# Sums of the exponentials in SBUF instead of PSUM, and a new hand-over to the list planner

## The chip, the cores and the metric

The kernel runs on one core of one Trainium2 chip. The metric is the device time of one execution in microseconds; the median over runs is given. TensorE (PE in the profile, PEld for its weight loads), VectorE (DVE), ScalarE (ACT), GpSimd (POOL) and the DMA queue of SyncE (SP) work side by side and wait for each other on semaphores.

## The reference, cut to what matters

Three layers follow each other. The first is attention on pooled keys and values (8 batches, 8 heads, 576 tokens, head size 64; 8 neighbouring keys are averaged, so 72 are left):

```
k_p = k.reshape(B, H, 72, 8, D).mean(axis=3); v_p = the same of v
scores = (q @ k_p^T) / 8;  scores -= max(scores)
attn = exp(scores);  attn /= (sum(attn) + 1e-9);  out = attn @ v_p
```

Its output, 4608 tokens of 512 numbers, passes two dense layers of 512 to 2048 to 512: `leaky(x @ w_in) @ w_out` with slope 0.01, and then `h * clip(h + 3, 0, 6) / 6` between two more such products. Each fp32 operand of these products is split into a high and a low part, so that three matmuls give one product.

## The kernel before, in words

The work is written as a list of tasks (`plan.add`, L130), each with an engine, an estimated cost in ns, a function that emits its instructions, and the views that it reads and writes. `Plan.order` (L211) makes each engine's instruction order out of it with a list schedule: twelve rounds forward and backward over the estimated costs and lags, of which the one with the earliest estimated end is kept. The estimates make the order alone; on the chip every wait is a semaphore. Copies among the first `flex` tasks (L303 to L314) may go to ACT or to DVE, as the schedule finds. `soon` (L1430) gives the first three weight chunks an earlier rank. Buffers of one tag rotate in the order in which the tasks are written down, whatever order the planner finds, and that is where the table `C` (L31) comes in: its `when`, `att`, `gaps`, `prep` and `left` numbers are slots, counted in steps of the dense layers, at which attention parts and weight preparation are written down between the steps.

Attention is done in 24 units, three per batch. A unit is, in this order: `scores` (L466: 24 or 32 small matmuls into two PSUM banks of tag `a`; the second unit's go to `y2` and `y3`), per bank a maximum on DVE (L503) and six exponentials on ACT (L512, 72 keys each, written to an SBUF tile `s` or `sb`), then 1e-9 added to the twelve sums (L523), their reciprocal (L524), and two products with it (L530 for the last 8 keys, L543 for the other 64). After that come `transposes` (L569) and `transpose_rem` (L587), whose results ACT and DVE split (`th`, `tl`, `rem`, `tr`), and `values` (L619), again into banks of tag `a`, of which there are two. Each exponential also writes the sum of its row (`accum_out`): in the profile that is a second ACT instruction, ACTIVATION_READ_ACCUMULATOR. Before the change it writes into columns 440 to 451 of the unit's first score bank.

The run has four parts. A ramp of some 35 us loads and pools keys and values and does the first two units; there the PE is kept running with matmuls on zeros (L1600, `idle`). Then the first dense layer takes three tiles of 512 tokens with plain products (`moe_tile`, L745 to L796), then three pairs of tiles (`Pair1`), then the second dense layer takes five pairs of 460 or 462 tokens. Both kinds of pair use seven products for eight (`Pair`, matmuls at L1049): 56 steps of six matmuls in `first`, then 56 steps in `second`, 112 slots in all. Their right sides are prepared by `prepare_some` (L1118), products 0 and 1 at one slot and 2 to 6 at another; their left sides are weights combined by DVE and ACT (`combine`, L948, `split_off`, L927) and kept in DRAM (`left`). The 24 units of attention are spread over the tiles and the first two pairs, and all have been done by 645 us. All loads and stores are issued from the one SP queue, in the planner's order.

Of the kernel before, what the change touches and what calls it, by code (L numbers as in the profile page):

```python
# [10 lines left out]
F32 = mybir.dt.float32  # L11
# [12 lines left out]
HALF, CQ, NC = 384, 128, 3  # L24
# [5 lines left out]
ROUNDS = 12  # L30
C = dict(  # L31
    n32=3,
    soon={0: 6000, 1: 6000, 2: 8000},
    flex=441,
    mid=8,
    half0=3,
    steps0='rfrfffrf',
    when0=[0, 2, 0, 8, 0, 10, 18],
    att0=[0, 14, 44],
    sec0=3,  # L40
    half1=3,
    steps1='frrfffrfffffffff',
    when1=[12, 20, 13, 22],
    att1=[0, 25, 31],
    sec1=3,
    att2=[7],
    quick=[0, 2, 0, 2, 3],
    slow=[0, 0, 5, 5, 3],
    left1=[[(0, 0), (1, 9)], [(2, 3), (3, 2)]],
    att3=[0, 5, 9, 12, 18, 22],  # L50
    gaps3=[0, 1, 1, 3, 2],
    prep3=[22, 31],
    att5=[9, 19, 32, 43, 54, 62],
    gaps5=[0, 4, 7, 9, 6],
    prep5=[82, 99],
    att7=[0, 16, 36],
    gaps7=[1, 10, 10, 12, 8],
    prep7=[72, 96],
    left2=[[(0, 11)], [(1, 15)], [(2, 27)], [(3, 39), (4, 43), (5, 61)], [(6, 17), (7, 30)]],
)  # L60
SCORES = 1500
EXPS = 1560
TRANSPOSES = 300
FIRST_LOADS = 1.25
WARM_FROM = 2700
ENGINES = ("pe", "act", "dve", "gp", "dma")
# [45 lines left out]
class Plan:  # L112
# [17 lines left out]
    def add(self, engine, cost, emit, reads=(), writes=(), other=None):  # L130

        n = len(self.tasks)
        after = set()
        over = lambda d, key: (t for k, v in d.items() if all(a == b for a, b in zip(k, key)) for t in v)
        for v in (*reads, *writes):
            assert not v.buf.gone, v.buf.name
            if v.buf.prev is not None:
                after |= v.buf.prev.users
        for v in reads:
            before = {t for key in v.keys for t in over(v.buf.writers, key)}  # L140
            assert before, v.buf.name
            after |= before
        for v in writes:
            for key in v.keys:
                after.update(over(v.buf.writers, key))
                after.update(over(v.buf.readers, key))
        after.discard(n)
        for v in reads:
            for key in v.keys:
                v.buf.readers.setdefault(key, set()).add(n)  # L150
            v.buf.users.add(n)
        for v in writes:
            for key in v.keys:
                v.buf.writers.setdefault(key, set()).add(n)
            v.buf.users.add(n)
        self.tasks.append(([(engine, cost, emit)] + ([other] if other else []), after))
# [97 lines left out]
def attention_moe_moe(ctx: ExitStack, tc: tile.TileContext, qt, kt, vm, vr, wt, wq, eye, mask, out):  # L254
# [14 lines left out]
    PE, ACT, DVE, GP, DMA = nc.tensor, nc.scalar, nc.vector, nc.gpsimd, nc.sync  # L269
    plan = Plan()  # L270
    add = plan.add

    def buf(tag, shape, dtype=F32, bufs=1, pool=sbuf):
        return Buf(plan, pool, tag, shape, dtype, bufs)
# [4 lines left out]
    def wide(ap, n):  # L279
        return ap.rearrange("p (a o) -> p a o", o=1).to_broadcast([ap.shape[0], ap.shape[1], n])  # L280
# [4 lines left out]
    def dve_cost(n, fast=False):  # L285
        return n / (1.92 if fast else 0.96) + 68
# [4 lines left out]
    def on_dve(n, emit, reads, writes, fast=False):  # L291
        add("dve", dve_cost(n, fast), emit, reads, writes)
# [4 lines left out]
    def on_pe(n, emit, reads, writes):  # L297
        add("pe", n, emit, reads, writes)
# [17 lines left out]
    def subtract(dst, a, b, n):  # L316
        on_dve(
            n,
            lambda: DVE.tensor_tensor(out=dst.ap(), in0=a.ap(), in1=f32(b.ap()), op=ALU.subtract),  # L319
            [a, b],  # L320
            [dst],
        )
# [9 lines left out]
    keys = [buf(f"keys{g}", [128, 2, SP])() for g in range(2)]  # L332
# [133 lines left out]
    def scores(u):  # L466


        assert all(held_keys[g] == u.b for g in u.groups)
        s = buf(u.tag, [128, 1024])  # L470
        u.rem = buf("rem", [CQ, NC, 3, 32], F32R, 2)
        mx = buf("mx", [CQ, NC, 4], F32, 2)
        at = lambda: s.get()[:, 0 : NC * 4 * SP].rearrange("p (c h k) -> p c h k", c=NC, h=4)
        tags = u.banks or [("a", 2), ("a", 2)]
        pss = [buf(tag, [128, 512], F32, bufs, psum) for tag, bufs in tags]
        if u.n == 2:
            blocks = [(slice(0, 128), c, c, 128 * c) for c in range(2)]
            blocks += [(slice(64 * g, 64 * g + 64), 2, g, 256 + 64 * g) for g in range(2)]
        else:
            blocks = [(slice(0, 128), c, u.g, 128 * c) for c in range(NC)]  # L480

        def emit():
            for to, c, g, at_ in blocks:
                for pi in range(2):
                    for e, ps in enumerate(pss):
                        rows = slice(64 * e, 64 * e + 64)
                        PE.matmul(
                            out=ps.get()[to, (2 * c + pi) * SP : (2 * c + pi) * SP + SP],
                            lhsT=u.q.ap()[rows, pi * HALF + at_ : pi * HALF + at_ + to.stop - to.start],
                            rhs=keys[g].ap()[rows, pi, :],  # L490
                            start=True,
                            stop=True,
                        )

        on_pe(SCORES, emit, [u.q, *(keys[g] for g in u.groups)], [ps("s") for ps in pss])
        sums = [pss[0](("m", e), lambda t, e=e: t[:, 440 + e : 452 + e]) for e in range(2)]
        for e, ps in enumerate(pss):
            s4 = lambda ps=ps: ps.get()[:, 0:432].rearrange("p (c a k) -> p c a k", c=NC, a=2)
            m = mx(e, lambda t, e=e: t[:, :, e : e + 3 : 2])

            on_dve(
                432,
                lambda m=m, s4=s4: DVE.tensor_reduce(out=m.ap(), in_=s4(), op=ALU.max, axis=AX.X, negate=True),  # L503
                [ps("s")],
                [m],
            )

            def exps(e=e, s4=s4):
                for c in range(NC):
                    for pi in range(2):  # L510
                        h = 2 * pi + e
                        ACT.activation(  # L512
                            out=at()[:, c, h, :],
                            in_=s4()[:, c, pi, :],
                            func=AF.Exp,
                            bias=mx.get()[:, c, h : h + 1],
                            accum_out=pss[0].get()[:, 440 + 4 * c + h : 440 + 4 * c + h + 1],
                        )

            add("act", EXPS, exps, [ps("s"), m], [s(e), sums[e]])  # L520
        whole = [s(pi) for pi in range(2)]
        inv = buf("inv", [CQ, 12], F32, 2)()
        on_dve(12, lambda: DVE.tensor_scalar_add(inv.ap(), pss[0].get()[:, 440:452], 1e-9), sums, [inv])  # L523
        add("dve", 144, lambda: DVE.reciprocal(out=inv.ap(), in_=inv.ap()), [inv], [inv])  # L524
        s3 = lambda: at().rearrange("p c h k -> p (c h) k")

        rn = buf("rn", [CQ, 12, 8], F32, 2)()
        on_dve(
            96,
            lambda: DVE.tensor_tensor(out=rn.ap(), in0=s3()[:, :, 64:SP], in1=wide(inv.ap(), 8), op=ALU.mult),  # L530
            [*whole, inv],
            [rn],
        )
        src = View(rn.buf, None, lambda t: t.rearrange("p (c h) k -> p c (h k)", c=NC))
        part = [u.rem(i, lambda t, i=i: t[:, :, i, :]) for i in range(3)]
        copy(part[0], src, 96)
        subtract(part[1], src, part[0], 96)
        copy(part[2], src, 96)

        flat = lambda: s.get()[:, 0 : NC * 256]  # L540
        on_dve(
            768,
            lambda: DVE.tensor_tensor(  # L543
                out=flat().rearrange("p (a k) -> p a k", k=64), in0=s3()[:, :, 0:64], in1=wide(inv.ap(), 64), op=ALU.mult
            ),
            [*whole, inv],
            whole,
        )
        u.p = lambda c, pi: flat()[:, 256 * c + 128 * pi : 256 * c + 128 * pi + 128]
        u.whole = whole  # L550
# [9 lines left out]
    def transposes(u):  # L560
        u.t = []
        pss = []
        for pi in range(2):
# [6 lines left out]

            on_pe(TRANSPOSES, emit, [*u.whole, ident], [ps()])
        for pi, ps in enumerate(pss):
# [9 lines left out]
    def transpose_rem(u):  # L582
# [9 lines left out]

        on_pe(TRANSPOSES, emit, [u.rem(), ident], [ps()])
        u.tr = buf("tr", [96, HALF], F32R, 1)()
# [46 lines left out]
    left1 = []  # L641
# [158 lines left out]
    class Jobs:  # L800
# [5 lines left out]
        def at(self, slot, *jobs):  # L806
            self.d.setdefault(slot, []).extend(jobs)
# [105 lines left out]
    left2 = Left(2)  # L913
# [487 lines left out]
    for u in units[: C["n32"]]:  # L1401
        g = u.n % 2
# [6 lines left out]
    for g in range(2):  # L1409
        for t in vbd[g]:  # L1410
            t = t()
# [251 lines left out]
```

## Time and profile before

| what | value |
|---|---|
| median of 3 runs | 1600.15 us (1599.05 to 1602.92) |
| time of the profiled execution | 1602.77 us |
| span of the profiled execution, first to last instruction | 1601.0 us |
| outside the span | 1.77 us |
| PE busy | 1575.8 us (98%) |
| DVE busy | 1159.1 us (72%) |
| ACT busy | 991.0 us (62%) |
| granted TensorE clock | 1.00 in every slice |

A busy PE is one with a matmul in flight; matmuls overlap, so busy time is not work. The chain that ended last is followed back from the last instruction, at each step to whatever released it. Idle time of an engine is listed with the instruction that ended it. In a timeline row the two first numbers are the start and the duration in us.

### The profile page before, as it was taken

How to read it: one execution, taken by the hardware profiler on the slowest of the kernel's cores; microseconds unless marked ns; L12 is line 12 of the kernel's file. 1: busy time of each engine (PE TensorE's matmuls, PEld its weight loads, DVE VectorE, ACT ScalarE, POOL GpSimd, SP SyncE). 2: the span in 40 equal slices, each digit the busy share in tenths (PEclk: the TensorE clock that was granted, in tenths of full speed). 3: DMA queues.
4: the chain of work that ended last, by engine and by line, in shares of the span. 5: the costliest groups of instructions: out<-in, count | busy, mean ns of one | idle time of the engine just before them, and what ended most of it. 6: DMA issues, size and time to landing. Idle time of an engine off the chain costs nothing.

```text
span 1601.0 us, 23002 instructions
## 1 busy us (share of the span) xinstructions
PE 1575.8 (98%) x8048; PEld 1348.6 (84%) x8048; DVE 1159.1 (72%) x2001; ACT 991.0 (62%) x2235; POOL 2.1 (0%) x12
## 2 busy tenths in 40 slices
PE   9999999999999999999999999999999999999999
PEld 8888878777787777778888889988888888898888
DVE  6987768568869966897577569658855955885494
ACT  7876765678876677666656455546545544654454
POOL 0000000000000000000000000000000000000000
PEclk9999999999999999999999999999999999999999
DMA  7789768649886799879987556856765685676564
GB/s 274 293 313 329 242 236 275 222 161 315 290 301 215 252 311 309 302 263 321 325 291 254 186 210 245 273 208 222 273 231 210 228 275 210 224 246 226 206 236 151
DMA packets 128323, 406.33 MB, mean 254 GB/s; under 512 B 18512, under 2 KB 47312, under 8 KB 106448
## 3 DMA queue, kind: packets, MB, share of 16 engines
q1 hardware_dynamic: 128208, 404.87, 73.2%
q8 instruction: 64, 1.05, 0.3%
q14 instruction: 51, 0.42, 0.1%
HBM read 317.79 MB, written 87.03 MB: 253 GB/s over the span
## 4 chain that ended last, share of the span: by engine, by line
PE 72%; DVE 12%; ACT 7%; DMA 6%; issue 2%; SPq 0%; ACTq 0%; DVEq 0%
PE y L1049 29%; PE h L1049 17%; PE a L1049 12%; ACT s L512 4%; DMA left<-st 3%; DVE w L916 2%; PE y L794 2%; PE y L796 2%; PE y L795 2%; PE a L619 2%; PE h L747 1%; PE h L746 1%; PE h L745 1%; DVE gl L319 1%; ACT sb L512 1%
## 5 line engine op out<-in xcount | busy, mean ns | idle before, releaser
L916 DVE TENSOR_TENSOR w<-y,w 128x512 f32<-128x512 f32 (+2 forms) x108 | 70.7, 659 | 105.4 <-PE y L1049 105.2
L312 ACT ACTIVATE gh<-w 128x460 fp32r<-128x460 f32 (+1 forms) x140 | 82.4, 589 | 65.4 <-PE y L1049 28.8
L916 DVE TENSOR_TENSOR w<-w 128x460 f32<-128x460 f32 (+2 forms) x168 | 105.5, 651 | 3.4 <-ACT w L760 3.1
L1244 DVE SCALAR_TENSOR_TENSOR gl<-w,gh 128x460 fp32r<-128x460 f32 (+1 forms) x140 | 89.2, 637 | 23.3 <-ACT gh L312 22.9
L1049 PE MATMUL y<-w,xh 128*128 128x512 f32 (+2 forms) x444 | 103.4, 383 | 1.2 <-ACT w L760 1.2
L1049 PEld LDWEIGHTS y<-w,xh 128*128 128x128 f32 x444 | 82.8, 188 | 14.8 <-ACT w L760 1.8
L794 PE MATMUL y<-gh,w 128*128 128x512 f32 (+2 forms) x216 | 84.4, 391 | 1.1 <-issue 1.1
L1215 ACT ACTIVATE gh<-w,three 128x460 f32<-128x460 f32 (+1 forms) x60 | 40.9, 682 | 70.6 <-DVE w L916 70.6
L1049 PE MATMUL y<-w,raw 128*128 128x460 f32 (+1 forms) x384 | 84.0, 372 | 0.0
L309 ACT CAST gh<-w 128x512 fp32r<-128x512 f32 x96 | 59.4, 622 | 38.3 <-PE y L1049 22.8
L745 PE MATMUL h<-xh,w 128*128 128x512 f32 (+2 forms) x216 | 81.5, 377 | 0.2 <-ACT u L760 0.2
L796 PE MATMUL y<-gh,w 128*128 128x512 f32 (+2 forms) x216 | 81.0, 375 | 0.0
L795 PE MATMUL y<-gl,w 128*128 128x512 f32 (+2 forms) x216 | 80.7, 374 | 0.1
L747 PE MATMUL h<-xh,w 128*128 128x512 f32 (+2 forms) x216 | 80.7, 373 | 0.0
L746 PE MATMUL h<-xl,w 128*128 128x512 f32 (+2 forms) x216 | 80.6, 373 | 0.0
L1049 PEld LDWEIGHTS y<-w,raw 128*128 128x128 f32 x384 | 72.1, 188 | 8.7
L1049 PE MATMUL y<-w,xl 128*128 128x512 f32 (+2 forms) x324 | 77.2, 386 | 0.0
L319 DVE TENSOR_TENSOR gl<-w,gh 128x512 fp32r<-128x512 f32 x96 | 66.0, 690 | 15.3 <-ACT gh L309 15.2
L309 ACT CAST st<-raw 128x512 fp32r<-128x512 f32 x88 | 54.4, 621 | 36.3 <-DMA left<-st 17.3
L512 ACT ACTIVATE s<-a,mx 128x72 f32<-128x72 f32 x204 | 65.4, 321 | 16.4 <-DVE mx L503 10.3
L319 DVE TENSOR_TENSOR st<-raw,st 128x512 fp32r<-128x512 f32 x88 | 60.2, 688 | 19.8 <-ACT st L309 19.3
L1049 PE MATMUL y<-gh,raw 128*128 128x462 f32 (+1 forms) x224 | 69.5, 371 | 0.0
(267 smaller groups left out, 4147.0 us busy)
## 6 DMA issues: line engine op xcount, KB each, us to landing
raw<-left SPq DMA_DIRECT2D x68, 1024.0 KB, 4.8
left<-st SPq DMA_DIRECT2D x176, 256.0 KB, 4.6
xh<-left SPq DMA_DIRECT2D x37, 1024.0 KB, 4.8
xl<-left SPq DMA_DIRECT2D x68, 512.0 KB, 5.0
xh<-left SPq DMA_DIRECT2D x56, 512.0 KB, 5.4
w<-left SPq DMA_DIRECT2D x56, 512.0 KB, 5.2
xl<-left SPq DMA_DIRECT2D x25, 1024.0 KB, 4.8
w<-wt SPq DMA_DIRECT2D x16, 1024.0 KB, 8.4
```

Source lines behind the costliest of these rows:

```text
L309: a = lambda: ACT.copy(out=dst.ap(), in_=src.ap())
L319: lambda: DVE.tensor_tensor(out=dst.ap(), in0=a.ap(), in1=f32(b.ap()), op=ALU.subtract),
L512: ACT.activation(out=at()[:, c, h, :], in_=s4()[:, c, pi, :], func=AF.Exp, bias=mx.get()[:, c, h : h + 1], accum_out=pss[0].get()[:, 440 + ...
L745: PE.matmul(out=o, lhsT=hi, rhs=xh.get()[:, k, c0:c1], start=k == 0, stop=False)
L746: PE.matmul(out=o, lhsT=hi, rhs=xl.get()[:, k, c0:c1], start=False, stop=False)
L747: PE.matmul(out=o, lhsT=lo, rhs=xh.get()[:, k, c0:c1], start=False, stop=k == 3)
L794: PE.matmul(out=y[:, n0:n1], lhsT=hi, rhs=gh.get()[:, n0:n1], start=start, stop=False)
L795: PE.matmul(out=y[:, c0:c1], lhsT=hi, rhs=gl.get()[:, c0:c1], start=False, stop=False)
L796: PE.matmul(out=y[:, c0:c1], lhsT=lo, rhs=gh.get()[:, c0:c1], start=False, stop=stop)
L916: on_dve(n, lambda: DVE.tensor_tensor(out=dst.ap(), in0=a.ap(), in1=b.ap(), op=op), [a, b], [dst])
L1049: PE.matmul(out=o, lhsT=l, rhs=r, start=first and i == m == 0, stop=last and i == len(left) - 1 and m == 2, skip_group_check=True,)
L1244: lambda: DVE.scalar_tensor_tensor(out=lo.ap(), in0=v.ap(), scalar=1.0 / 6.0, in1=f32(hi.ap()), op0=ALU.mult, op1=ALU.subtract),
```

## The change

Three things. The twelve sums of a unit go to an SBUF tile `sm` of 128 x 12 with two buffers, instead of the first score bank; L523 reads them there. In the task list the score banks are then whole views, and the sums are views of `sm`. The planner's cost of a block of scores goes from 1500 to 1600 ns, of six exponentials from 1560 to 1782, of three transposes from 300 to 260. And the table `C` has other slots.

```
 C = dict(
     n32=3,
-    soon={0: 6000, 1: 6000, 2: 8000},
-    flex=441,
+    soon={0: 2000, 1: 4000, 2: 4000},
+    flex=561,
...
-    steps0='rfrfffrf',
-    when0=[0, 2, 0, 8, 0, 10, 18],
-    att0=[0, 14, 44],
-    sec0=3,
+    steps0='rfrffffr',
+    when0=[0, 0, 6, 4, 6, 4, 12],
+    att0=[0, 11, 50],
+    sec0=4,
...
-    when1=[12, 20, 13, 22],
-    att1=[0, 25, 31],
+    when1=[11, 22, 15, 23],
+    att1=[0, 26, 31],
...
-    quick=[0, 2, 0, 2, 3],
-    slow=[0, 0, 5, 5, 3],
-    left1=[[(0, 0), (1, 9)], [(2, 3), (3, 2)]],
-    att3=[0, 5, 9, 12, 18, 22],
-    gaps3=[0, 1, 1, 3, 2],
-    prep3=[22, 31],
-    att5=[9, 19, 32, 43, 54, 62],
-    gaps5=[0, 4, 7, 9, 6],
-    prep5=[82, 99],
-    att7=[0, 16, 36],
-    gaps7=[1, 10, 10, 12, 8],
-    prep7=[72, 96],
-    left2=[[(0, 11)], [(1, 15)], [(2, 27)], [(3, 39), (4, 43), (5, 61)], [(6, 17), (7, 30)]],
+    quick=[0, 1, 0, 2, 0],
+    slow=[0, 2, 5, 5, 2],
+    left1=[[(0, 7), (1, 8)], [(2, 6), (3, 2)]],
+    att3=[0, 5, 8, 10, 17, 27],
+    gaps3=[0, 1, 0, 2, 2],
+    prep3=[30, 47],
+    att5=[11, 18, 32, 43, 54, 62],
+    gaps5=[0, 6, 2, 9, 3],
+    prep5=[78, 118],
+    att7=[0, 19, 35],
+    gaps7=[1, 12, 11, 12, 6],
+    prep7=[80, 87],
+    left2=[[(0, 11)], [(1, 19)], [(2, 32)], [(3, 55), (4, 36), (5, 54)], [(6, 20), (7, 44)]],
 )
-SCORES = 1500
-EXPS = 1560
-TRANSPOSES = 300
+SCORES = 1600
+EXPS = 1782
+TRANSPOSES = 260
...
-        on_pe(SCORES, emit, [u.q, *(keys[g] for g in u.groups)], [ps("s") for ps in pss])
-        sums = [pss[0](("m", e), lambda t, e=e: t[:, 440 + e : 452 + e]) for e in range(2)]
+        on_pe(SCORES, emit, [u.q, *(keys[g] for g in u.groups)], [ps() for ps in pss])
+        sm = buf("sm", [CQ, 12], F32, 2)
...
-                            accum_out=pss[0].get()[:, 440 + 4 * c + h : 440 + 4 * c + h + 1],
+                            accum_out=sm.get()[:, 4 * c + h : 4 * c + h + 1],
...
-            add("act", EXPS, exps, [ps("s"), m], [s(e), sums[e]])
+            add("act", EXPS, exps, [ps(), m], [s(e), sm(e)])
...
-        on_dve(12, lambda: DVE.tensor_scalar_add(inv.ap(), pss[0].get()[:, 440:452], 1e-9), sums, [inv])
+        on_dve(12, lambda: DVE.tensor_scalar_add(inv.ap(), sm.get(), 1e-9), [sm()], [inv])
```

## Rows read from the trace of the kernel before

**Rows 1.** The page: its head and the busy time of PE.

```profile
span 1601.0 us, 23002 instructions
...
PE 1575.8 (98%) x8048; PEld 1348.6 (84%) x8048; DVE 1159.1 (72%) x2001; ACT 991.0 (62%) x2235; POOL 2.1 (0%) x12
```

**Rows 2.** Busy time by stretch: bounds, length, busy us by engine, clock, DMA.

```profile
0.00:40.00 40.00, 36.43 (x406) 33.20 (x406) 27.45 (x53) 29.25 (x101) 1.91 (x11) 1.00 0.78 274
40.00:690.00 650.00, 632.17 (x3409) 520.01 (x3410) 499.75 (x872) 466.01 (x1267) 0.20 (x1) 1.00 0.80 272
690.00:1600.00 910.00, 907.23 (x4234) 795.37 (x4232) 631.88 (x1077) 495.72 (x870) 0.00 (x0) 1.00 0.69 240
```

**Rows 3.** Waits of PE, 40 to 690 us: total us, times, longest us.

```profile
PE a L587 <- DVE tl L319: 3.2, 4, 0.9
PE a L569 <- DVE sb L543: 3.2, 3, 1.6
PE y L1049 <- ACT w L309: 2.1, 2, 1.7
PE a L569 <- DVE s L543: 2.1, 3, 0.9
PE a L619 <- ACT s L512: 2.1, 1, 2.1
PE y L1049 <- ACT w L760: 1.2, 1, 1.2
...
PE a L569 <- ACT u L760: 0.9, 1, 0.9
```

**Rows 4.** Timeline of ACT, 10 to 15 us: start us, duration us, instruction.

```profile
10.07 0.32 ACT L512 ACTIVATE s<-a,mx 128x72 f32<-128x72 f32 x1 [1.36 <-DVE mx L503]
10.29 0.16 ACT L512 ACTIVATION_READ_ACCUMULATOR s<-a,mx 128x1 f32 x1
10.48 0.32 ACT L512 ACTIVATE s<-a,mx 128x72 f32<-128x72 f32 x1
...
14.84 0.16 ACT L512 ACTIVATION_READ_ACCUMULATOR s<-a,mx 128x1 f32 x1
14.89 0.32 ACT L512 ACTIVATE sb<-y,mx 128x72 f32<-128x72 f32 x1
```

**Rows 5.** The DVE instructions on the sums: min, median, max ns.

```profile
L523 DVE TENSOR_SCALAR inv<-a x23: 170/171/172, 15.0 to 634.5; 128x12 f32<-128x12 f32 x23
```

**Rows 6.** DVE's reciprocal of the same size, out of SBUF.

```profile
L524 DVE RECIPROCAL inv<-inv x24: 210/228/229, 15.6 to 634.7; 128x12 f32<-128x12 f32 x24
```

**Rows 7.** The chain that ended last, 0 to 42 us: shares by line.

```profile
by line: ACT s L512 21.3%; PE idle L1600 17.5%; PE h L410 7.9%; DVE w L310 6.8%; ACT sb L512 4.8%; issue 4.8%; PE a L619 4.2%; PE a L487 3.7%; DVE mx L503 2.9%; DVE w L672 2.7%; DVE w L319 2.7%; DVE w L664 2.7%; ACT w L661 2.5%; PE a L587 2
```

**Rows 8.** Timeline of ACT and PE, 487 to 493 us, where a value product waits.

```profile
487.23 0.32 ACT L512 ACTIVATE s<-a,mx 128x72 f32<-128x72 f32 x1 [0.59 <-DVE mx L503]
489.76 0.40 PE L1049 MATMUL y<-gh,xl 128*128 128x512 f32 x1
492.23 0.45 PE L619 MATMUL a<-th,vbd 128*128 128x384 f32 x1 [2.07 <-ACT s L512]
```

**Rows 9.** DMA issues: count, KB each, median us to landing.

```profile
w<-wt SPq DMA_DIRECT2D x16, 1024.0 KB, 8.4
```

**Rows 10.** Busy time by stretch around the end of the first pair.

```profile
480.00:520.00 40.00, 37.93 (x205) 31.02 (x205) 37.82 (x66) 27.86 (x72) 0.00 (x0) 1.00 0.63 214
520.00:560.00 40.00, 39.68 (x172) 31.88 (x171) 36.00 (x62) 24.39 (x45) 0.00 (x0) 1.00 0.75 250
```

**Rows 11.** A piece of the chain in a pair: start us, us, twelve matmuls.

```profile
493.93 2.79 PE y L1049 x12
```

**Rows 12.** Groups by line: count, busy us, mean ns of one, idle before.

```profile
L916 DVE TENSOR_TENSOR w<-w 128x460 f32<-128x460 f32 (+2 forms) x168 | 105.5, 651 | 3.4 <-ACT w L760 3.1
```

**Rows 13.** The same view with shapes apart: ACT copies out of SBUF and PSUM.

```profile
L309 ACT CAST st<-raw 128x512 fp32r<-128x512 f32 x88 | 54.4, 621 | 36.3 <-DMA left<-st 17.3 <-DVE raw L916 14.0 <-DVE raw L672 3.3
L309 ACT COPY w<-y 128x512 f32<-128x512 f32 x48 | 27.5, 591 | 10.1 <-PE y L1049 10.1
```

More of the change, by code (lines that the diff above doesn't have):

```diff
@@ L503, in scores @@
                 lambda m=m, s4=s4: DVE.tensor_reduce(out=m.ap(), in_=s4(), op=ALU.max, axis=AX.X, negate=True),
-                [ps("s")],
+                [ps()],
                 [m],
```

## The prediction

> **What bounds the kernel now.** First the page's head: PE is busy 1575.8 of 1601.0 us [rows 1]. Busy time by stretch tells where the rest lies [rows 2]. From 690 us to the end PE is busy 907.23 of 910 us, so there the matmuls alone set the time. All attention lies before. From 40 to 690 us PE idles 650 - 632.17 = 17.8 us, and in the ramp before 40 us it runs largely on zeros. So nothing can be won but these 17.8 us and part of the ramp.
>
> Next the waits of PE in that stretch [rows 3]. Two kinds are seen. Attention's own: L587 for `tl` 3.2 us, L569 for the normalised exponentials 3.2 and 2.1, L619 for a block of exponentials 2.1, L569 for `u` (ACT late) 0.9; together 11.5 us in 13 waits, the longest 2.1. The other kind is dense work (`w` late by ACT): 2.1, 1.2, and some smaller ones. No DMA ends a wait in these rows.
>
> Then the timeline of the exponentials [rows 4]. The sum is read out 0.22 us after its exponential has begun (10.07 to 10.29) and takes 0.16, so it is over at 10.45; the next exponential begins at 10.48, just behind it. Where the next one belongs to another unit, with another bank for its sums, it begins 0.05 us after the read-out has begun (14.84 to 14.89), and so overlaps most of it. The engine can thus overlap the two; inside a unit something holds the next one back. Each one reads or writes the bank into which the read-out writes, so I take it for a wait on that bank.
>
> **The change part by part.**
>
> *Sums in SBUF.* A unit's twelve exponentials now last from 10.07 to 14.89 = 4.82 us [rows 4]. If the sums' columns in SBUF hold nobody back, one lasts 0.22 + 0.05 = 0.27 us, twelve 3.24, and a unit is 1.58 us shorter. That is the upper end. The lower end is nothing: if the wait comes from elsewhere, the rhythm of 0.41 stays. The diff's own new estimate, 1782 for six, would be 3.56 us for twelve, a gain of 1.26. The row of the overlapped pair is the nearest one, the same two instructions on the same engine; I take 1.4 us, between it and the estimate. 24 units make 34 us of ACT time. ACT is busy 466 of 650 us [rows 2], so this counts only where someone waits for it.
>
> *In the ramp* someone does. The chain up to 42 us holds 21.3% + 4.8% of exponentials [rows 7], that is 0.261 x 42 = 10.96 us. At 0.297 us (1782/6) for 0.41 each, 3.0 us go; at 0.27, 3.7. The lower end is 0, since the same chain runs through the decoding of weights on DVE (L310, L319, L664, L672 and L661 on ACT), which may then end last, all the more as `soon` gives the first three chunks less precedence. I take 3.0, as the exponentials are the largest share of that chain.
>
> *In 40 to 690 us* the exponentials stand ahead of L543 and L569, and each block shuts ACT to the copies that PE waits for, `th` (and with it `tl`) among them. The mean wait of attention is 11.5/13 = 0.9 us, the longest 2.1; a unit shortened by 1.4 us covers the mean. In the old list six exponentials stood with 1560 ns while they took 2.41 (half of 4.82), so that ACT ran 0.85 us later than planned at each of 48 blocks; in the new one estimate and duration come near each other. I take two thirds of the 11.5 us, 7.7. Ends: 0, if the new order has as many waits elsewhere; all 17.8 us that PE idles.
>
> *The bank set free earlier.* At 492.23 us a value product waits 2.07 us for the last of twelve exponentials that began at 487.23 [rows 8]: its buffer is the first score bank of the next unit, which held the sums until all twelve and L523 were over. With `sm` that bank is free after six, 6 x 0.297 = 1.8 us after 487.23, before the PE's last matmul at 489.76. Only batch 6 is written down that way (scores of its third unit at slot 62, values of the second at 54 + 9 = 63); after the change it still is. It is the 2.1 us inside the 11.5.
>
> *Reading the sums on DVE.* L523 takes 171 ns out of PSUM [rows 5], a reciprocal of the same size out of SBUF 228 [rows 6]. So it may move by some 57 ns either way, 24 x 0.057 = 1.4 us of DVE in all, hidden by DVE's idle quarter; taken as 0. The tile itself adds no instruction, and its two buffers are read long before they come round again.
>
> *Costs of scores and transposes, new slots, `flex`.* They shorten no instruction; they move work. On the SP queue the weight loads and the `left` stores move with their slots; a load takes 8.4 us at most in the median [rows 9], and weights for the later parts are made long ahead, so I count 0; without that cover it is one such landing. `flex` lets 120 more tasks choose DVE, which is busier than ACT (499.75 against 466.01 us [rows 2]); 0, hidden by the quarter of DVE that is idle. The parts after 690 us keep their matmuls: 0.
>
> *Sum.* 3.0 + 7.7 = 10.7 us. The profiled execution took 1602.77 us, its span 1601.0 and 1.77 around it; it would take 1592.1. It lies 2.6 above the median of the runs shown, so that the forecast for the median is 1600.15 - 10.7 = 1589.4 us.
>
> **The rivals.**
>
> *The order gives it back* (or the wait stays). The exponentials get shorter, but what PE waits for in 40 to 690 us moves to DVE, which is busier than ACT; the ramp ends on the decoding. Or the next exponential waits for the read-out in SBUF too, and the change is then only another order. For: in [rows 3] DVE is named as releaser in most of attention's waits. Against: those DVE steps come behind ACT's blocks. Time: 1600 us, give or take 3.
>
> *Slower: a late second pair.* `prep5`'s second slot goes from 99 to 118, behind the last of the pair's 112 slots. Products 2 to 6 of the next pair's right sides are then written down behind everything of the first pair: per half 4 differences and 5 low parts on DVE, 18 in all, at 0.651 us [rows 12] 11.7 us of DVE. The first of them is due two products after the next pair begins, which is 4 x 6 matmuls or 5.6 us at 2.79 per twelve [rows 11]. DVE is nearly full there, 37.82 and 36.00 of 40 us [rows 10]. If the planner's order follows the slots, PE waits 11.7 - 5.6 = 6 us, and with what else DVE owes there about 10; with the ramp's 3 us gained that is 1607. It decides from the point where DVE has over some 4 us of additional work between 500 and 560 us. Against: DVE's place goes by due time, not by slot.
>
> *Slower: sums reach SBUF later than PSUM.* If the wait stays and each read-out takes longer, ACT loses. The nearest rows are ACT's 512-column copies, 621 ns out of SBUF and 591 out of PSUM [rows 13]: 30 ns. 288 read-outs make 8.6 us, and if all of it falls on PE, 1609. The Trainium skill, page "ScalarE: Activation LUTs", section "Step-by-step: what each stage is for", says that ScalarE writes to PSUM with less latency than to SBUF, so that by it the old place is the better one; it gives no figure, and no row here shows a sum written to SBUF.
>
> **How the numbers follow.** The forecast's case, faster by some 6 to 20 us, 0.70; the order gives it back, 0.19, of which 0.04 is that the wait stays; the late second pair 0.08; the slower read-out 0.03. A measurement of this kernel can tell about 0.3% or 4.8 us from no change, that is 1595.3 to 1605.0. So faster 0.70, same 0.19, slower 0.11. The range goes from 1600.15 - 3.7 - 17.8 = 1578.7, taken as 1579, the case in which every idle of PE up to 690 us and the ramp's upper end are won, to 1603, the end of the case without a gain. Beyond it lie the two slower rivals, 0.11, and some of the tail below.
>
> **What would show it.** Exponentials begin 0.27 to 0.30 us apart for 0.41, and a unit's twelve take 3.2 to 3.6 us; ACT is busy for 0.27 to 0.30 us per exponential where it was for 0.38 (10.07 to 10.45), so that its busy time falls by 288 x 0.08 to 0.11, 23 to 32 us, from 991. In the chain up to 40 us their share falls, and the first dense matmul comes some 3 us earlier. The waits of L569, L587 and L619 fall from 11.5 to about 4 us; the one of 2.1 us on exponentials is gone. From 690 us on nothing changes but the offset. Wrong it would be if the exponentials stay 0.41 us apart, if attention's waits vanish and as many of dense work appear, or if PE idles at the start of the second pair.

## The result, and the profile after

The changed kernel takes 1579.97 us (median of 4 runs, 1578.43 to 1580.9) against 1599.6 us for the kernel before in the same comparison: ratio 0.9873, interval 0.9856 to 0.9890, so 19.6 us or 1.3% less. The forecast was 10.7 us less. The direction and the range hold, but the time lies only 1 us inside the range's fast end of 1579, the case in which every idle microsecond is won; the size is 1.8 times the forecast.

The page's head and its chain line, after, which answer to [rows 1], and last the chain line before:

```profile
span 1579.1 us, 22961 instructions
...
PE 1570.8 (99%) x8030; PEld 1349.6 (85%) x8030; DVE 1158.9 (73%) x2001; ACT 973.6 (62%) x2235; POOL 2.1 (0%) x12
...
PE 93%; DMA 4%; DVE 2%; ACT 1%; issue 0%; SPq 0%; ACTq 0%; DVEq 0%
```

```profile
PE 72%; DVE 12%; ACT 7%; DMA 6%; issue 2%; SPq 0%; ACTq 0%; DVEq 0%
```

The chain that ended last is now PE's own for 93% of the span, where it was for 72%. Busy time by stretch, with the columns of [rows 2]:

```profile
0.00:40.00 40.00, 38.07 (x405) 34.66 (x406) 30.47 (x58) 29.99 (x108) 1.91 (x11) 1.00 0.83 293
40.00:690.00 650.00, 647.15 (x3481) 535.85 (x3480) 512.78 (x894) 461.39 (x1285) 0.20 (x1) 1.00 0.82 280
```

In 40 to 690 us PE idles 650 - 647.15 = 2.9 us, where it idled 17.8. All waits of PE that the view still lists in that stretch (total us, times, longest; [rows 3]):

```profile
PE a L619 <- DVE tl L319: 0.9, 1, 0.9
PE a L487 <- DVE tl L319: 0.9, 1, 0.9
PE a L569 <- ACT tr L309: 0.5, 1, 0.5
```

Attention's 11.5 us are 2.3, and the dense layers' waits for `w` are gone as well. The timeline of ACT answers to [rows 4]:

```profile
10.03 0.32 ACT L512 ACTIVATE s<-a,mx 128x72 f32<-128x72 f32 x1 [1.54 <-DVE mx L503]
10.25 0.19 ACT L512 ACTIVATION_READ_ACCUMULATOR s<-a,mx 128x1 f32 x1
10.34 0.31 ACT L512 ACTIVATE s<-a,mx 128x72 f32<-128x72 f32 x1
...
10.64 0.32 ACT L512 ACTIVATE s<-a,mx 128x72 f32<-128x72 f32 x1
...
13.59 0.38 ACT L512 ACTIVATE sb<-y,mx 128x72 f32<-128x72 f32 x1
```

The next exponential begins 0.09 us after the read-out has begun, not behind its end. Exponentials are 0.30 us apart, and the twelve of unit 0 take 13.59 - 10.03 = 3.56 us for 4.82. The trace also holds the wait itself. In the kernel before, 272 of the 288 exponentials wait for a semaphore that the read-out ahead of them sets, on their own engine; in the changed kernel 2 do. So it is a wait of the program, and since each sum had a column of its own, it goes by the whole buffer, which is one bank, as the prediction took it. Whether the chip needs it there, no run tried. Of the ramp, one row before and one after, the first dense matmul:

```profile
34.62 0.42 PE L745 MATMUL h<-xh,w 128*128 128x384 f32 x1
```

```profile
30.88 0.44 PE L745 MATMUL h<-xh,w 128*128 128x384 f32 x1
```

It comes 3.7 us earlier. With 17.8 - 2.9 = 14.9 us of idle time that makes 18.6 us. The profiled executions differ by 1602.77 - 1580.9 = 21.9 us (the one before lies 3.2 us above its median, the one after 0.9), so 3.3 us of this pair are in neither term. Part of them may be that a wait costs more than the idle time: the matmul behind the wait of [rows 8] takes 0.45 us, the same one in e1, without a wait, 0.34.

### The profile page after: what moved, and what is told of

Same layout as the page of the kernel before. It is cut to its first block, busy times and chain, and to the rows that moved or that the text cites. A ratio compares the mean times of both kernels' runs of the same rounds, so it can differ in the third digit from the quotient of the medians.

```text
span 1579.1 us, 22961 instructions
## 1 busy us (share of the span) xinstructions
PE 1570.8 (99%) x8030; PEld 1349.6 (85%) x8030; DVE 1158.9 (73%) x2001; ACT 973.6 (62%) x2235; POOL 2.1 (0%) x12
## 4 chain that ended last, share of the span: by engine, by line
PE 93%; DMA 4%; DVE 2%; ACT 1%; issue 0%; SPq 0%; ACTq 0%; DVEq 0%
PE y L1049 35%; PE h L1049 21%; PE a L1049 13%; PE h L745 3%; PE y L794 3%; PE h L747 3%; PE h L746 3%; PE y L795 3%; PE y L796 3%; PE a L619 2%; PE a L487 2%; DMA raw<-wq 1%; DMA raw<-vr 1%; DMA raw<-vm 1%; PE idle L1600 1%; PE a L569 1%
## 5 line engine op out<-in xcount | busy, mean ns | idle before, releaser
L1049 PE MATMUL y<-w,xh 128*128 128x512 f32 (+2 forms) x444 | 103.5, 382 | 0.0
L1049 PEld LDWEIGHTS y<-w,xh 128*128 128x128 f32 x444 | 82.8, 188 | 12.9
L1049 PE MATMUL y<-w,raw 128*128 128x460 f32 (+1 forms) x384 | 83.4, 370 | 0.0
L1049 PEld LDWEIGHTS y<-w,raw 128*128 128x128 f32 x384 | 72.1, 188 | 8.2
L1049 PE MATMUL y<-w,xl 128*128 128x512 f32 (+2 forms) x324 | 78.2, 391 | 0.0
L309 ACT CAST st<-raw 128x512 fp32r<-128x512 f32 x87 | 54.3, 628 | 33.0 <-DMA left<-st 17.4
L319 DVE TENSOR_TENSOR st<-raw,st 128x512 fp32r<-128x512 f32 x88 | 60.1, 686 | 15.7 <-ACT st L309 14.9
L1049 PEld LDWEIGHTS y<-w,xl 128*128 128x128 f32 x324 | 61.5, 191 | 11.0
L1049 PE MATMUL y<-gh,raw 128*128 128x462 f32 (+1 forms) x224 | 70.0, 373 | 0.0
```

The costliest lines, as they stand in the source:

```text
L309: a = lambda: ACT.copy(out=dst.ap(), in_=src.ap())
L1049: PE.matmul(out=o, lhsT=l, rhs=r, start=first and i == m == 0, stop=last and i == len(left) - 1 and m == 2, skip_group_check=True,)
```

## The experiments

**Theories.** A: the length of a block of exponentials is the cause, in whatever order. B: the new order, made with lengths that fit, is the cause. Each kernel ran on the same chip as the kernel before; ratios are to it.

**e1: the sums moved, the order untouched.** The task list keeps its old views, so that every engine's order is that of the kernel before; only the emitted addresses differ.

```
-        sums = [pss[0](("m", e), ...) for e in range(2)]
+        sm, sums = buf("sm", [CQ, 12], F32, 2), [pss[0](("m", e), ...) for e in range(2)]
...
-                            accum_out=pss[0].get()[:, 440 + 4 * c + h : 440 + 4 * c + h + 1],
+                            accum_out=sm.get()[:, 4 * c + h : 4 * c + h + 1],
...
-        on_dve(12, lambda: DVE.tensor_scalar_add(inv.ap(), pss[0].get()[:, 440:452], 1e-9), sums, [inv])
+        on_dve(12, lambda: DVE.tensor_scalar_add(inv.ap(), sm.get(), 1e-9), sums, [inv])
```

> The sums go to SBUF, each engine's order stays that of the kernel before, instruction for instruction. Theory A (what matters is the length of a block of exponentials): they begin 0.295 us apart for 0.415, the first dense matmul comes 2 to 4 us earlier, attention's waits of PE fall from 11.5 us to under 4, and the time falls by 10 to 16 us, to 1584 to 1590. Theory B (what matters is an order made with estimates that fit): the block gets as short, but PE's order was made for other lengths, and under 6 us are gained, 1594 or more.

Measured: 1582.09 us, ratio 0.9877 (0.9862 to 0.9893). That is the changed kernel's ratio to within the intervals, and more than theory A expected. Busy time of 40 to 690 us in e1, and its largest waits of PE there:

```profile
40.00:690.00 650.00, 645.74 (x3474) 533.37 (x3474) 511.53 (x892) 458.69 (x1284) 0.21 (x1) 1.00 0.82 280
```

```profile
PE h L1049 <- ACT w L309: 1.4, 1, 1.4
PE a L569 <- DVE sb L543: 1.0, 1, 1.0
PE a L587 <- DVE tl L319: 0.6, 1, 0.6
```

The same order, and PE idles 4.3 us for 17.8. The last matmul of attention, in the kernel before and in e1:

```profile
679.13 0.27 PE L619 MATMUL a<-tr,vrm 96*128 96x192 f32 x1
```

```profile
658.45 0.27 PE L619 MATMUL a<-tr,vrm 96*128 96x192 f32 x1
```

It comes 20.7 us earlier, and the spans differ by 1601.0 - 1579.4 = 21.6 us, so the gain is there when attention ends. (The value products of the kernel before end at 679 us, not by 645 as said ahead; 690 us still lies behind them.) The bank set free earlier is seen as well, in the timeline of e1 at the place of [rows 8]:

```profile
475.07 0.37 ACT L512 ACTIVATE s<-a,mx 128x72 f32<-128x72 f32 x1
475.27 0.34 PE L619 MATMUL a<-th,vbd 128*128 128x384 f32 x1
...
475.37 0.38 ACT L512 ACTIVATE s<-a,mx 128x72 f32<-128x72 f32 x1
```

The value product runs between two exponentials of the second block and waits for nothing, where it stood 2.07 us for the last of them.

**e2: the new order, the sums back in PSUM.** The order of the changed kernel, instruction for instruction.

```
-                            accum_out=sm.get()[:, 4 * c + h : 4 * c + h + 1],
+                            accum_out=pss[0].get()[:, 440 + 4 * c + h : 440 + 4 * c + h + 1],
...
-        on_dve(12, lambda: DVE.tensor_scalar_add(inv.ap(), sm.get(), 1e-9), [sm()], [inv])
+        on_dve(12, lambda: DVE.tensor_scalar_add(inv.ap(), pss[0].get()[:, 440:452], 1e-9), [sm()], [inv])
```

> The order of the changed kernel, instruction for instruction, but the sums back in the first score bank, so that the exponentials are 0.415 us apart again. Theory A: most of the gain is lost, 1594 to 1606, with waits of PE behind exponentials and in the ramp. Theory B: the new order keeps most of it, 1582 to 1590.

Measured: 1600.63 us, ratio 0.9990 (0.9980 to 1.0000). Busy time of 40 to 690 us: PE idles 13.9 us.

```profile
40.00:690.00 650.00, 636.08 (x3423) 524.06 (x3422) 501.61 (x876) 468.69 (x1269) 0.21 (x1) 1.00 0.81 273
```

With e1 this decides between A and B for this change: the sums' place carries the gain, and the new order with its table adds none that can be measured, neither with long blocks (e2 against the kernel before) nor with short ones (the changed kernel against e1). In the ramp it does move something: the first dense matmul begins at 31.98 us in e2, 2.6 us earlier than before with blocks as long, and yet the time is hardly shorter.

**e5: one column in SBUF for all sums of a block.** The changed kernel in its own order, with the wait put back and the place kept.

```
-                            accum_out=sm.get()[:, 4 * c + h : 4 * c + h + 1],
+                            accum_out=sm.get()[:, e : e + 1],
...
-        ... DVE.tensor_scalar_add(inv.ap(), sm.get(), 1e-9) ...
+        ... DVE.tensor_scalar_add(inv.ap(), sm.get()[:, 0:1].to_broadcast([CQ, 12]), 1e-9) ...
```

> The changed kernel, its order unchanged, but the six sums of a block go into one and the same SBUF column, and the reciprocal is taken of the first column for all twelve (so the rows are not normalised by their own sums). If the rhythm of 0.415 us comes of each read-out being waited for, it comes back in SBUF (0.42 to 0.46 us apart, as the read-out is longer there), and the time is that of e2 within 4 us. If it came of PSUM itself, the exponentials stay 0.295 us apart and the time stays at 1580.

Measured: 1599.5 us, ratio 0.9983 (0.9973 to 0.9992), within 1.2 us of e2. The timeline of ACT in e5, and the read-outs in e5 and in e2 (min, median, max ns):

```profile
10.12 0.32 ACT L512 ACTIVATE s<-a,mx 128x72 f32<-128x72 f32 x1
10.34 0.19 ACT L512 ACTIVATION_READ_ACCUMULATOR s<-a,mx 128x1 f32 x1
10.56 0.32 ACT L512 ACTIVATE s<-a,mx 128x72 f32<-128x72 f32 x1
...
L512 ACT ACTIVATION_READ_ACCUMULATOR s<-a,mx x204: 188/193/223, 9.9 to 630.9; 128x1 f32 x102
```

```profile
L512 ACT ACTIVATION_READ_ACCUMULATOR s<-a,mx x204: 160/163/191, 9.6 to 630.9; 128x1 f32 x102
```

In SBUF, with a common column, the exponentials are 0.44 us apart, and 242 of the 288 wait for the read-out's semaphore. So what costs is that each waits for the read-out before it, not PSUM as such. The read-out itself is 30 ns longer in SBUF (193 for 163).

**e6 and e7: the ramp's units and the others.** As e1, with the SBUF sums for batch 0 alone (`u.b == 0`, three units), and for batches 1 to 7 alone (`u.b > 0`, 21 units).

```
+                            accum_out=sm.get()[:, ...] if u.b == 0 else pss[0].get()[:, 440 + ...],
...
+        ... DVE.tensor_scalar_add(inv.ap(), sm.get() if u.b == 0 else pss[0].get()[:, 440:452], 1e-9) ...
```

> Sums in SBUF for the three units of batch 0 alone (the ramp's exponentials and the first block of the tiles), in PSUM for the other 21; every engine's order is that of the kernel before. By the prediction's term for the ramp 3.0 to 3.7 us are gained. If a gain early in the run is lost again at the next wait, under 1 us is left.

Measured: 1599.18 us, ratio 0.9986 (0.9976 to 0.9997), 2.2 us less than before, 0.5 to 3.8. The first dense matmul begins at 31.58 us, 3.0 earlier than before.

> The reverse: sums in SBUF for the 21 units of batches 1 to 7, in PSUM for batch 0; order of the kernel before. By the prediction's term 7.7 us, at most 11.5. If the waits of the dense layers between 40 and 690 us also come of ACT being late behind exponentials, 14 to 17 us, and with e6 the sum of both is that of e1, about 20.

Measured: 1580.83 us, ratio 0.9874 (0.9852 to 0.9895), 20.2 us less, 16.8 to 23.7: more than either expectation. Busy time of 40 to 690 us in e6, then in e7:

```profile
40.00:690.00 650.00, 630.72 (x3389) 517.40 (x3388) 495.92 (x866) 462.70 (x1259) 0.21 (x1) 1.00 0.81 271
```

```profile
40.00:690.00 650.00, 647.90 (x3487) 535.29 (x3487) 512.82 (x893) 460.85 (x1289) 0.20 (x1) 1.00 0.83 280
```

PE idles 19.3 us in e6 and 2.1 in e7. The ramp's part is small, and the prediction's 3.0 lies within its interval. Whether it comes on top of e7's is not decided: e1 has both and is no faster than e7 within the intervals.

**e8 and e9: ACT held for as long as before.** As e1, but behind each unit's twelve exponentials ACT copies a 128 x 256 scratch tile onto itself, three times in e8, once in e9. Nothing in the program makes the normalisation on DVE depend on these copies.

```
+            def exps_pad(e=e, exps=exps):
+                exps()
+                if e == 1:
+                    for _ in range(3):
+                        ACT.copy(out=held_pad[0], in_=held_pad[0])
...
-            add("act", EXPS, exps, [ps("s"), m], [s(e), sums[e]])
+            add("act", EXPS, exps_pad, [ps("s"), m], [s(e), sums[e]])
```

> The sums in SBUF and the order of the kernel before, as in e1, but behind the twelve exponentials of each unit ACT makes three idle copies of 256 columns, about 1.3 us, so that ACT is held for as long as before the change while the unit's own chain to the normalisation is short. If what counts is that chain (the waits of transposes), most of e1's 20 us stay: 1583 to 1588. If what counts is how long ACT is shut to the copies that PE waits for, most goes: 1592 to 1600.

Measured: 1599.1 us, ratio 0.9982 (0.9972 to 0.9993). The copies in e8, and its largest waits of PE (lines stand 7 further down than in the kernel before, L576 for L569, L594 for L587, L1056 for L1049):

```profile
L525 ACT COPY padin<-padin 128x256 f32<-128x256 f32 x72 | 30.8, 428 | 1.5
```

```profile
PE a L594 <- DVE tl L319: 3.3, 4, 0.9
PE a L576 <- DVE sb L550: 3.3, 3, 1.4
PE a L576 <- DVE s L550: 2.5, 4, 0.7
PE y L1056 <- ACT w L309: 1.8, 2, 1.5
PE y L1056 <- ACT w L767: 1.3, 1, 1.3
```

30.8 us of copies that compute nothing bring back 17 us (0.9982 against e1's 0.9877), and the list of waits is that of [rows 3] again, dense ones included, but for L619's wait on exponentials. In each unit DVE begins on the sums as soon after the first exponential as in e1. The chain to the normalisation did not stay short, though, as the expectation had it. One unit in e1, then the same unit in e8 (L550 for L543), rows of ACT and then of DVE:

```profile
350.47 0.69 ACT L309 CAST gh<-u 128x512 fp32r<-128x512 f32 x1
...
351.32 0.69 DVE L319 TENSOR_TENSOR gl<-u,gh 128x512 fp32r<-128x512 f32 x1
351.92 0.95 DVE L543 TENSOR_TENSOR s<-s,inv 128x768 f32<-128x768 f32 x1
```

```profile
361.16 1.35 ACT L525 COPY padin<-padin 128x256 f32<-128x256 f32 x3
362.42 0.62 ACT L309 CAST gh<-u 128x512 fp32r<-128x512 f32 x1
...
363.07 0.69 DVE L319 TENSOR_TENSOR gl<-u,gh 128x512 fp32r<-128x512 f32 x1 [0.96 <-ACT gh L309]
363.68 0.95 DVE L550 TENSOR_TENSOR s<-s,inv 128x768 f32<-128x768 f32 x1
```

On ACT the cast `gh` of a dense layer stands behind the copies, on DVE the subtraction `gl` waits for it, and the normalisation stands behind `gl`. Counted from the first exponential, it ends 0.9 to 1.2 us later than in e1 in 15 of the 24 units, and as in e1 in the other nine. So e8 shows what ACT's time is worth in this order, but it does not tell that time from the unit's chain.

> As e8, with one idle copy of about 0.43 us behind each unit's exponentials instead of three, so that ACT keeps two thirds of the time that the sums' move sets free. If the loss goes with ACT's time, a third of e8's loss of 17 to 20 us, that is 1586 to 1590. If it is a step (only a copy past some point costs anything), 1582 or 1599.

Measured: 1584.22 us, ratio 0.9898 (0.9883 to 0.9914).

```profile
L525 ACT COPY padin<-padin 128x256 f32<-128x256 f32 x24 | 11.3, 470 | 0.0
```

11.3 us of copies cost 3.4 us against e1, the other 19.5 us of e8 cost 13. The time lies between the two cases expected. The intervals of e9 and e1 overlap, so neither a loss in proportion (some 6 us) nor a cheaper first third is shown.

**e10: DVE held.** As e1, ACT free; DVE works on a scratch tile between the sums and the reciprocal.

```
...
+            DVE.tensor_scalar_add(inv.ap(), sm.get(), 1e-9)
+            for _ in range(3):
+                DVE.tensor_scalar_add(held_pad[0], held_pad[0], 0.0)
...
```

> Sums in SBUF and the order of the kernel before, as in e1; ACT stays free, but DVE makes three idle operations of 450 columns behind the twelve sums of each unit, 1.0 to 1.3 us, ahead of the reciprocal, so that the unit's chain to the normalisation is as long as before the change. If only ACT's time counts, it is e1's time within 3 us, 1579 to 1585. If the unit's chain or DVE's time counts as well (DVE is busy for 77% of that stretch), 1588 to 1600.

Measured: 1596.62 us, ratio 0.9970 (0.9961 to 0.9980). The operations, and the largest waits of PE (here L575 for L569, L593 for L587):

```profile
L527 DVE TENSOR_SCALAR padin<-padin 128x450 f32<-128x450 f32 x72 | 28.4, 394 | 1.6
```

```profile
PE a L575 <- DVE sb L549: 3.6, 3, 1.5
PE a L593 <- DVE tl L319: 2.8, 4, 1.0
PE a L575 <- DVE s L549: 2.6, 4, 0.7
```

28.4 us on DVE bring back 15 us. So it is not ACT alone; here DVE's time and the unit's chain were lengthened together, and the run doesn't tell them apart. Of e1's 20 us some 3 are left with ACT held (e8) and 5 with DVE held (e10): a delay of about a microsecond in each unit costs most of the gain on either engine.

**e4 and e12: the kernel before with the length it really has.** One number is changed, the planner's cost of six exponentials, in PSUM and with the old table.

```
-EXPS = 1560
+EXPS = 2420
```

> The kernel before with one number changed: the planner's cost of six exponentials is 2420 ns, what they take in its trace, for 1560. The sums stay in PSUM. Theory A: the blocks are as long as before and the ramp gains nothing, 1593 to 1603. Theory B: an order that knows the length loses little, 1583 to 1590.

Measured: 1591.13 us, ratio 0.9937 (0.9919 to 0.9954). e12 has 2500 there.

> As e4 (sums in PSUM, old table), with the cost of six exponentials at 2500 for 2420: the same knowledge of the length, another order. If e4's 10 us come of the planner's knowing the length, 1588 to 1594; if they were the luck of one order, anywhere from 1588 to 1604.

Measured: 1591.3 us, ratio 0.9935 (0.9917 to 0.9954). Busy time of 40 to 690 us in e4, then in e12:

```profile
40.00:690.00 650.00, 642.85 (x3474) 531.43 (x3471) 507.87 (x894) 469.18 (x1272) 0.20 (x1) 1.00 0.81 278
```

```profile
40.00:690.00 650.00, 642.57 (x3484) 532.40 (x3483) 508.88 (x889) 471.67 (x1280) 0.21 (x1) 1.00 0.81 277
```

PE idles 7.2 and 7.4 us for 17.8, with exponentials still 0.415 us apart. Both lie between what theory A and theory B expected of e4. Two different orders give the same 10 us, so this is hardly the luck of one. An order that knows the long block hides half of what the block costs. Theory B is right about that, but it is not what this change did: its estimate of 1782 fits the short block. In e1 the shorter block also comes nearer to the old estimate, 1770 ns (6 x 0.295 us) for 1560 where it took 2.41 us; how much of e1's gain is that, no run tells.

**e3 and e11: other orders for short blocks.** e3 is the changed kernel with the old table `C`; e11 is the changed kernel with `EXPS = 1800`.

> Sums in SBUF and the new costs of scores, exponentials and transposes, but the old table of slots: the order is made anew. If an order made with fitting lengths is worth something by itself once the blocks are short, this is 2 to 4 us faster than e1, about 1578. If PE has hardly anything left to wait for, it is e1's time within 2 us.

Measured: 1585.74 us, ratio 0.9898 (0.9881 to 0.9916), slower than both expectations, though its interval overlaps that of e1.

> The changed kernel with the planner's cost of six exponentials at 1800 ns for 1782: another order, nothing else. If an order's fit to the table of slots matters, this scatters by several us, 1580 to 1588; if PE has next to nothing left to wait for in any sensible order, 1578 to 1582.

Measured: 1578.5 us, ratio 0.9858 (0.9844 to 0.9873). e11 is the fastest of all, but its interval overlaps that of the changed kernel, so it is not shown to beat it. The first dense matmul and the busy time of 40 to 690 us in e3:

```profile
34.59 0.42 PE L745 MATMUL h<-xh,w 128*128 128x384 f32 x1
```

```profile
40.00:690.00 650.00, 646.56 (x3481) 534.63 (x3482) 512.27 (x895) 459.77 (x1286) 0.20 (x1) 1.00 0.83 279
```

and the same in e11:

```profile
29.54 0.42 PE L745 MATMUL h<-xh,w 128*128 128x384 f32 x1
```

```profile
40.00:690.00 650.00, 647.10 (x3485) 534.84 (x3484) 513.28 (x897) 457.40 (x1286) 0.20 (x1) 1.00 0.82 281
```

Past the ramp PE idles as little in both as in the others with short blocks, 3.4 and 2.9 us. The ramp differs: e3's first dense matmul comes 5 us behind e11's, and no earlier than the 34.62 us of the kernel before, short blocks or not. Four orders with short blocks, e1, the changed kernel, e3 and e11, lie between 0.9858 and 0.9898, some 6 us apart, and the intervals of e3 and e11 do not meet. So an order can still be worth some microseconds, in the ramp.

## Why the prediction was right in sign and short in size

*What bounds it: right.* All but about 1 us of what was won in e1 is there when attention ends: PE's idle time up to there, and the earlier start of the dense layers.

*Sums in SBUF: right.* 1.26 us less per unit; taken were 1.4, ends 0 and 1.58. Twelve take 3.56 us, which is what the diff's own estimate gives. That inside a unit the exponential waits for the read-out was inferred from one pair of rows; e5 shows it, by bringing the wait back in SBUF, and so do the semaphores in the trace.

*In the ramp: right in size, by e6.* Taken 3.0. With the order unchanged and short blocks in batch 0 alone, the first dense matmul comes 3.0 us earlier and the run is 2.2 (0.5 to 3.8) us shorter. The 3.7 of the changed kernel's profile are not the exponentials' alone: its order brings 2.6 with long blocks too (e2). That the term adds to the next one is not shown, since e7 does without it and is as fast as e1.

*In 40 to 690 us: this term was mis-sized,* 7.7 us for 14.9. It has two parts. Of attention's 11.5 us it took two thirds, without giving a reason for the share; 2.3 are left, so 9.2 went. The other 17.8 - 11.5 = 6.3 us of PE's idle time, `w` late by ACT above all, it put at nothing, though it had named them among PE's waits; 0.6 are left, so 5.7 went. By time, the 21 units outside batch 0 are worth 20.2 us (16.8 to 23.7), by e7. The prediction had the mechanism for attention: each block shuts ACT to the copies that PE waits for. The same holds for the dense layers' `w`, and that it left out: in e1 and e7 these waits are gone or smaller though no order changed, and in e8 they are back with ACT's copies. Of the 34 us of ACT's time it said that they count "only where someone waits for it"; by e8 31 such microseconds are worth 17, about half, although ACT was busy for only 72% of that stretch. e8's rows show one way: a copy that is late on ACT holds what stands behind it on DVE, the normalisation included. What share goes by that way and what share by PE's own waits for ACT stays open.

The reading behind the term has a slip: the waits listed as attention's are 12, not 13, so their mean is 0.96 us. Nothing else hangs on it.

*"Hidden by DVE's idle quarter": not a safe reason.* It was said of 1.4 us and of `flex`, and there nothing came of it. But e10 puts 28.4 us on DVE, in the middle of the units' chains, and loses 15 us. An engine's idle quarter does not by itself hide work.

*The bank set free earlier: right,* seen in e1's timeline.

*Estimates that fit: half right.* The prediction took ACT's being 0.85 us late at each block for a cause of the waits. e4 and e12 show that an order that knows the length is worth 10 us when blocks are long. With short blocks no more of it can be seen, since the changed kernel is no faster than e1, whose order was made for 1560.

*The rivals.* "The order gives it back" fell: e1, e3, e11 and the changed kernel are four orders, and all gain 15 us or more. Its other half, that the wait stays in SBUF, fell with the rhythm of 0.295 us. The late second pair did not come: among all the waits of PE that are left in 40 to 690 us there is none of L1049, the pairs' line. The read-out to SBUF is slower by the very 30 ns that the prediction took from its nearest rows. The Trainium skill, page "ScalarE: Activation LUTs", section "Step-by-step: what each stage is for", says that ScalarE's way to PSUM is the quicker one, and e5 against e2 agrees, 193 ns against 163. It does not decide here, because the wait that the sums' place in PSUM brought with it, 0.12 us per exponential, is four times as long.

*What the profile would show.* Rhythm, ramp and waits came as written. ACT's busy time fell by 991.0 - 973.6 = 17.4 us, less than the 23 to 32 that were worked out; the exponentials' own records get longer (last section).

## What to carry to other kernels

Before counting freed time as hidden, price it: add it back as idle work on the same engine, in the same order, and look in the trace at what else the idle work delays. Here ACT was busy for 72%, and 31 us of its time were worth 17 us of a run that is bound by PE. Look at the gap between an instruction and its successor of the same kind: a successor that starts just behind the end, where other pairs overlap, may be waiting on a shared buffer. Here a small separate tile with a column for each removed the wait, and the semaphores in the trace named it. And separate a change of order from a change of length by emitting the one in the other's order; here the length carried the gain, and the new order none that could be measured, though with the sums left in PSUM an order that knew the long blocks (e4) was worth half as much.

## What the runs showed of the hardware that was not expected

Exponentials that overlap get longer in the records from one to the next. In the changed kernel (min, median, max ns):

```profile
L512 ACT ACTIVATE s<-a,mx x204: 302/342/401, 10.0 to 612.1; 128x72 f32<-128x72 f32 x102
L512 ACT ACTIVATION_READ_ACCUMULATOR s<-a,mx x204: 190/230/289, 10.2 to 612.3; 128x1 f32 x102
```

Before, and in e5, where each waits for the last, the median exponential takes 321 ns. The first of a block still takes 0.32 us and the first read-out 0.19; in the timeline above the one at 13.59 takes 0.38. The rhythm stays at 0.295 us (median), and it is this that sets the time. The two rows of the overlapped pair in [rows 4] had suggested 0.27. The read-out into SBUF is 30 ns longer (e5 against e2), which is near the 0.025 us of difference; that it is the cause was not tried.
